# GpSimd's weight sums read the low parts from SBUF, and direct parts go to DRAM in the second plain block

## The chip, the core and the metric

The kernel runs on one core of one Trainium2 chip. The metric is the device time of one execution in microseconds (us); the median of several runs is compared. The engines are named as in the profile: PE is TensorE, ACT ScalarE, DVE VectorE, POOL GpSimd and SP SyncE, whose queue issues nearly all transfers here.

## The reference

```python
def _attn_ref(q, k, v):            # 8 x 8 heads, 576 tokens, 64 wide
    B, H, S, D = q.shape
    chunk = 64
    nc = S // chunk
    ...
    scores = scale * np.matmul(q_c, k_c.transpose(0, 1, 2, 4, 3))   # per chunk of 64
    scores = scores - np.max(scores, axis=-1, keepdims=True)
    attn = np.exp(scores)
    attn = attn / (np.sum(attn, axis=-1, keepdims=True) + 1e-09)
    out = np.matmul(attn, v_c)
...
def _moe_ref(x, w_in, w_out):      # x (4608, 512), w_in (512, 2048), w_out (2048, 512)
    h = x @ w_in
    g = np.where(h > 0.0, h, alpha * (np.exp(np.minimum(h, 0.0)) - 1.0))
    return (g @ w_out).astype(np.float32)
```

An attention within chunks of 64 tokens makes the 4608 x 512 matrix x; two matrix products with an ELU between them follow. The weights arrive as float64 words and are used as a high and a low float32r part, and x and g are split in the same way, so that each product is made of three matmuls (high by high, high by low, low by high).

## The kernel before

**Blocks.** The 4608 tokens are nine blocks of 512. The first three are computed plainly, block by block: for each of 16 column blocks f, h is computed (12 matmuls), put through the ELU, split, and multiplied with the rows f of w_out (12 matmuls). The other six blocks are taken two at a time, in three superblocks s = 0, 1, 2. In a superblock the first product is done by a scheme with seven products in place of eight: for each of eight pairs g of column blocks (2g and 2g + 1) the string PAIR lists the products (p1 to p7), their evacuations and sums (c, d), the steps of the ELU (digits), second products (Q), the steps of the attention of later tokens (m, E, z, h, q, k, s, v, x) and their loads (l, V). The first token block's half of g is used at once; the other half is kept in g_kept and multiplied with w_out afterwards, in the 16 rows of KEPT ("the second half-block"), where also the inputs of the next superblock are prepared (items beginning with x). The last superblock uses a scheme with seven products for w_out too.

**Order.** All engines work in the order in which the program issues to them; the strings are that order, written out by hand. An instruction that waits holds back all that stands behind it on its engine, and a transfer that waits holds back SP.

**The weights.** The operands for the seven products of w_in are written once to DRAM (a_dram, in `combine()`, during the second plain block) and loaded again for each pair (`load_a`, the profile's wi_hi<-a_dram; seven of 256 KB a pair). The high part of w_out stays in SBUF. Of the low part, from the third plain block on, only a ring of four slots is in SBUF, `weights[0][3]` (named wo_lo in the profile), each slot holding the low rows of two column blocks; `load_lo` reloads a slot of 512 KB from lo_dram, the copy in DRAM, once the second column block of the slot has been used, so that slot g is in the ring when pair g begins.

**Operands for the last superblock.** The seven operands made of w_out lie in b_dram. Three of them (A11, A12, A22) are plain parts of w_out. `write_direct` copies them in twelve transfers of 512 KB: six from SBUF (high parts, the profile's b_dram<-wo_hi) and six from lo_dram (low parts, DRAM to DRAM). The item w at the end of PAIR issues one of them per pair. The other four are sums. `Combination` makes them in 16 units (eight pairs g, two column halves m): load the low part from lo_dram into the tile quad (256 KB, line 556), add the high part on GpSimd (128x512), four sums of 128x128 on GpSimd (line 559), cast on ScalarE (line 572), subtract on VectorE (line 575), two writes to b_dram (line 581). Each item b in a string takes one of seven steps; the first 14 units are spread over the pairs of superblocks 0 and 1, the rest over KEPT of superblock 1 and the first pair of superblock 2.

The split of a kept column block (`split_kept`) casts on ScalarE and subtracts on GpSimd, except for column blocks 0 and 15, where VectorE subtracts.

Of the kernel before, what the change touches and what calls it, by code (L numbers as in the profile page):

```python
# [1 line left out]

# [1 line left out]

# [16 lines left out]
def kernel(  # L21
# [293 lines left out]
    class Later:  # L315


        def __init__(self, n: int):
            self.n = n
# [208 lines left out]
    HALF = DM // 2  # L528
    NM = HALF // P
    b_dram = dram.tile([NG, P, len(BOPS), 2, HALF], F32, name="b_dram")  # L530
    DIRECT = {"A11": (0, 0), "A12": (1, 0), "A22": (1, 1)}

    def write_direct(half: int, name: str, lo: int):
# [5 lines left out]
                "g p d -> p g d"),  # L539
            in_=src[:, :, e * DM + dh * HALF:e * DM + (dh + 1) * HALF])  # L540

    def quad_hi():
        return flat(weights[0][0])[:, NA * 4 * P:(NA + 1) * 4 * P]

    class Combination:

        def __init__(self, n: int):
            self.g, self.m = divmod(n, NM)
            half, f = divmod(2 * self.g, NF // 2)
            self.hi, self.lo = [  # L550
                w.rearrange("p (i m c) -> p i m c", i=4, m=NM)[:, :, self.m]
                for w in (flat(weights[half][2]).bitcast(F32)[:, f * DM:(f + 2) * DM],
                          lo_dram[half][:, f * DM:(f + 2) * DM])]

        def load(self):
            nc.sync.dma_start(out=quad, in_=self.lo)

        def pool(self, out, a, b, op):
            nc.gpsimd.tensor_tensor(out=out, in0=a, in1=b, op=op)  # L559

        def combine(self):
            a11, a21, a12, a22 = [quad[:, i] for i in range(4)]
            self.pool(quad, self.hi, quad, ALU.add)
            yield
            self.pool(a22, a21, a22, ALU.add)
            self.pool(a21, a11, a21, ALU.subtract)
            yield
            self.pool(a11, a22, a11, ALU.subtract)
            self.pool(a12, a12, a11, ALU.subtract)

        def cast(self):
            nc.scalar.copy(out=quad_hi(), in_=flat(quad))

        def subtract(self):
            nc.vector.tensor_tensor(
                out=flat(quad).bitcast(F32R), in0=flat(quad), in1=quad_hi().bitcast(F32),
                op=ALU.subtract)

        def write(self):
            for lo, src in enumerate((quad_hi().bitcast(F32), flat(quad))):  # L580
                nc.sync.dma_start(
                    out=b_dram[self.g, :, 3:, lo, self.m * P:(self.m + 1) * P],
                    in_=src.rearrange("p (i c) -> p i c", i=4))

    def combinations():
        for n in range(NG * NM):
            unit = Combination(n)
            unit.load()
            yield
            yield from unit.combine()  # L590
            yield
            for step in (unit.cast, unit.subtract, unit.write):
                step()
                yield

    def load_b(j: int):
        i, g = b_order[j]
# [201 lines left out]

    def split_kept(f: int):  # L800

        if f < NF - NTT or not preparing:
            hi, lo = [flat(weights[1][3])[:, (2 * (f % NTT) + i) * TB:(2 * (f % NTT) + i + 1) * TB]
                      for i in range(2)]
        else:
            hi, lo = g_tiles()
        for _ in split_g(g_place(f), hi, lo, nc.vector if f in (0, NF - 1) or not preparing and f % 2 == 0 else nc.gpsimd):
            pass
        second(f, hi, lo)

# [25 lines left out]
    def warm(n: int):  # L836
# [51 lines left out]
        "3 3"  # L888
    )
    SECOND_PAIR = (  # L890
        "p1 c1 5 5 h Q 4 p2 d1 4 Q q k p6 c2 1 Q Q 1 p5 1 1 Q l p7 c3 d2 Q Q 2 p4 c4 2 Q b 3 p3 "
        "d3 3 3 3 s v x V"
    )
    PAIR = (
        "b b b m p1 c1 4 E Q 4 z p2 d1 Q p6 c2 b h b 1 Q Q 1 p5 1 q k 1 b Q l p7 c3 d2 Q Q b 2 p4 c4 "
        "2 Q 3 p3 d3 3 3 3 s v x V w"
    )
    LAST_FIRST = (
        "b b b p1 c1 Q Q p2 d1 Q Q b b b p6 1 c2 Q p5 1 1 1 Q p7 c3 d2 Q Q 2 p4 c4 2 3 p3 d3"
    )  # L900
    LAST = (
        "5 4 p1 c1 Q 5 p2 4 t1 d1 Q 5 p6 1 t2 c2 p5 1 t3 1 1 th tl t4 p7 c3 d2 Q Q 2 p4 c4 2 3 p3 "
# [10 lines left out]
    )  # L913
    KEPT = (
# [145 lines left out]
    for f in range(NF):  # L1060
        tt, st = divmod(f, 4)
        n = 2 * NTT + tt + 1
        if st == 0:
            tile_now = following
            next(tile_now, None)
            next(tile_now, None)
            if tt == 0:
                later[n] = Later(n)
                later[n].load_qk()
            later[n].load_v()  # L1070
            following = later[n].steps()
        for item in (LATER if tt else SECOND_BLOCK)[st].split():
            if item == "H":
                act, acted = elu(hidden(f)), 0
            elif item == "e":
                g, acted = next(act), acted + 1
                if acted == 4:
                    second(f, *g)
            elif item == "a":
                next(tile_now, None)  # L1080
            elif item == "n":
                next(following, None)
            elif item == "X":
                if f == NF - 1:
                    split_next()
            elif item == "P":
                second_products()
            elif item == "S":
                store(*unstored.pop())
        if f < 2:  # L1090
            write_lo(NF - 2 + f)
        next(combining, None)
        if st == 2:
            later[n + 1] = Later(n + 1)
            later[n + 1].load_qk()
# [5 lines left out]
    def do(item: str):  # L1101
        if item == "Q":
            second_next()
        elif item == "b":
            next(combinations_next, None)
        elif item == "P":
            second_products()
        elif item == "S":
            store(*unstored.pop())
        elif item[0] == "x" and len(item) > 1:  # L1110
            if preparing:
                name, cols = item[1:3], slice(TB)
                if item[1] == "B":
                    name = item[1:4]
                elif item[3:4] in ("a", "b"):
                    cols = slice(T2) if item[3] == "a" else slice(T2, TB)
                prepare(name, cols)
# [5 lines left out]
    preparing = True  # L1123
# [20 lines left out]
    combinations_next = combinations()  # L1144
    direct_writes = iter([(half, name, lo) for half in range(2) for name in DIRECT for lo in range(2)])
# [50 lines left out]
    def pair_step(item: str, before):  # L1196
        if item[0] == "p":
            pair.product(int(item[1]))
        elif item[0] == "c":
            pair.keep(int(item[1]))  # L1200
        elif item[0] == "d":
            pair.add(int(item[1]))
        elif item in "45":
            if before:
                next(before.parts["3" if item == "5" else item], None)
        elif item in "123":
            next(pair.parts[item])
        elif item[0] == "t":
            before.combine(item[1])
        elif item == "w":  # L1210
            for what in [next(direct_writes, None)]:
                if what:
                    write_direct(*what)
        else:
            return False
        return True

    for s in range(NS):
# [5 lines left out]
        for g in range(NG):  # L1224
            before, pair = pair, Pair(s * NG + g)
            order = PAIR
            if last:
                order = LAST_FIRST if g == 0 else LAST_LAST if g == NG - 1 else LAST
            elif not s and g < 2:
                order = (FIRST_PAIR, SECOND_PAIR)[g]  # L1230
# [4 lines left out]
                    do(item)  # L1235
        if last:
            break
        preparing, kept = s + 2 <= NS - 1 or s + 1 < NS, iter(range(NF))
        run = n0 + TB, o_tiles(), b_half_place
        for line in KEPT:  # L1240
            for item in line.split():
                if item == "4":
                    next(pair.parts["4"], None)
                elif item == "G":
                    split_kept(next(kept))
                elif item == "B":
                    if s == NS - 2:
                        next(combinations_next, None)
                else:
                    do(item)  # L1250

# [48 lines left out]
```

## Time and profile before

| | us |
|---|---|
| median of 3 runs (lowest to highest) | 886.84 (886.29 to 888.61) |
| the profiled execution: time | 883.31 |
| its span, first to last instruction | 881.2 |
| TensorE busy | 831.8 (94%) |
| VectorE, ScalarE, GpSimd busy | 567.4, 506.4, 208.8 |
| granted TensorE clock over the span | 0.975 |

Some stretches of the span, as the trace shows them: start and attention of the first tokens to 28, the first plain block to 130, the second to 228, the third to 323, the pairs of superblock 0 to 478 and its KEPT to 523, the pairs of superblock 1 to 675 and its KEPT to 718, the last superblock to the end.

In a row of the trace "out<-in" names the tile written and the tile read, xN is the number of instructions merged, and the bracket at the end is the idle time before the instruction and what ended it. A row of a table by stretch gives the stretch and its length, then the busy time and number of instructions of each engine, the granted clock (1.00 is full), the mean busy share of the 16 DMA engines and the rate in GB/s. A row of waits gives who waited for whom, the total in us, the number of times and the longest. A row of a line or tile of SP gives the duration in ns (least, median, most) of issuing, and the times of the first and last.

### The profile page before, as it was taken

What the parts mean: (1) busy time and instruction counts of PE and PEld (TensorE: products, weight loads), DVE (VectorE), ACT (ScalarE), POOL (GpSimd) and SP (SyncE); (2) the same over time, 40 slices, a digit from 0 to 9 for tenths busy, and PEclk for the clock granted to TensorE, in tenths of its full rate; (3) what the DMA queues carried; (4) which work ended last, traced back from release to release, by engine and by line L of the source; (5) the groups of instructions that cost most, each with busy time, mean ns of one, the idle gap of its engine ahead of it and who ended that gap; (6) DMA issues with size and microseconds to landing.
All of it is one profiled execution on the core that took longest, in us unless ns stands there. A gap on an engine that the chain in (4) does not pass through costs nothing.

```text
span 881.2 us, 16030 instructions
## 1 busy us (share of the span) xinstructions
PE 831.8 (94%) x5901; PEld 674.4 (77%) x5901; DVE 567.4 (64%) x820; ACT 506.4 (57%) x910; POOL 208.8 (24%) x209
## 2 busy tenths in 40 slices
PE   6899999999899999698989999799899999999997
PEld 5787887888688878576867888577678888888886
DVE  4999986666755787454655766455555646777744
ACT  6999975444544457364645436445556447777641
POOL 0000004555012121222323463232224930000000
PEclk9999999999999999898999999989899999999999
DMA  9947965776785976599999868789987547665576
GB/s 248 274 149 228 297 146 167 239 233 194 230 212 153 239 187 207 156 279 254 264 259 262 250 165 251 222 245 255 262 242 215 172 134 242 195 193 158 153 211 150
DMA packets 231981, 189.29 MB, mean 215 GB/s; under 512 B 83936, under 2 KB 210400, under 8 KB 231904
## 3 DMA queue, kind: packets, MB, share of 16 engines
q1 hardware_dynamic: 229792, 188.01, 75.5%
q8 instruction: 47, 0.77, 0.4%
q10 hardware_dynamic: 2112, 0.26, 0.2%
q14 instruction: 30, 0.25, 0.1%
HBM read 144.70 MB, written 42.99 MB: 213 GB/s over the span
## 4 chain that ended last, share of the span: by engine, by line
PE 63%; DMA 11%; issue 9%; SPq 6%; ACT 5%; DVE 3%; POOL 3%; ACTq 0%; POOLq 0%
PE o L406 32%; PE h L406 27%; DMA b_dram<-lo_dram 3%; DMA quad<-lo_dram 2%; DMA wi_hi<-a_dram 2%; SPq L213 2%; POOL glo L441 2%; PE ps_a L233 1%; DMA b_dram<-wo_hi 1%; SPq L197 1%; PE ps_a L241 1%; POOL quad L559 1%; SPq L625 1%; DMA v_sb<-in_v_dram 1%; ACT unturned L367 1%
## 5 line engine op out<-in xcount | busy, mean ns | idle before, releaser
L406 PE MATMUL h<-xhi,wi_hi 128*128 128x512 f32 x324 | 116.3, 422 | 30.5 <-ACT kept L747 24.9
L406 PE MATMUL o<-wo_hi,ghi 128*128 128x512 f32 x352 | 140.8, 400 | 0.3 <-ACT k_sb L446 0.3
L406 PE MATMUL o<-wo_hi,glo 128*128 128x512 f32 x352 | 139.1, 395 | 1.1 <-DVE glo L441 0.6
L406 PE MATMUL o<-wo_lo,ghi 128*128 128x512 f32 x352 | 138.8, 394 | 0.0
L406 PE MATMUL h<-xlo,wi_hi 128*128 128x512 f32 x324 | 110.3, 402 | 0.0
L406 PEld LDWEIGHTS h<-xhi,wi_hi 128*128 128x128 f32 x324 | 63.8, 200 | 48.6 <-ACT kept L747 35.1
L682 POOL TENSOR_TENSOR glo<-e,ghi 128x512 fp32r<-128x512 f32 x32 | 41.4, 1293 | 167.8 <-ACT ghi L680 167.8
L406 PEld LDWEIGHTS o<-wo_hi,glo 128*128 128x128 f32 x352 | 67.1, 191 | 17.1 <-DVE glo L441 1.6
L406 PEld LDWEIGHTS o<-wo_hi,ghi 128*128 128x128 f32 x352 | 67.0, 190 | 15.2 <-ACT k_sb L446 0.4
L406 PEld LDWEIGHTS o<-wo_lo,ghi 128*128 128x128 f32 x352 | 67.1, 191 | 13.6
L406 PE MATMUL h<-wi_lo,wi_hi 128*128 128x512 f32 x288 | 75.1, 396 | 0.0
L406 PEld LDWEIGHTS h<-xlo,wi_hi 128*128 128x128 f32 x324 | 64.3, 199 | 13.9
L406 PE MATMUL h<-wo_lo,wi_hi 128*128 128x512 f32 x288 | 71.8, 389 | 0.0
L406 PE MATMUL o<-wo_hi,wo_lo 128*128 128x512 f32 x240 | 71.0, 390 | 0.0
L406 PE MATMUL h<-xhi,wi_lo 128*128 128x512 f32 x180 | 70.2, 390 | 0.0
L747 ACT COPY kept<-h 128x512 f32<-128x512 f32 x72 | 42.0, 583 | 40.9 <-PE h L406 40.7
L675 DVE SCALAR_TENSOR_TENSOR g_kept<-e,g_kept 128x512 f32<-128x512 f32 x48 | 34.9, 727 | 44.7 <-ACT e L672 44.7
L406 PEld LDWEIGHTS h<-wo_lo,wi_hi 128*128 128x128 f32 x288 | 54.0, 188 | 11.2
L672 ACT ACTIVATE e<-e 128x512 f32<-128x512 f32 x96 | 60.7, 632 | 3.1
L406 PEld LDWEIGHTS h<-wi_lo,wi_hi 128*128 128x128 f32 x288 | 52.9, 188 | 11.6 <-DVE g_kept L751 0.3
L406 PE MATMUL o<-wo_lo 128*128 128x512 f32 x192 | 59.9, 389 | 0.0
L751 DVE TENSOR_TENSOR g_kept<-h,kept 128x512 f32<-128x512 f32 x48 | 33.0, 688 | 36.8 <-PE h L406 30.1
(160 smaller groups left out, 1569.1 us busy)
## 6 DMA issues: line engine op xcount, KB each, us to landing
wi_hi<-a_dram SPq DMA_DIRECT2D x168, 256.0 KB, 4.3
wo_lo<-lo_dram SPq DMA_DIRECT2D x36, 512.0 KB, 5.6
wo_lo<-b_dram SPq DMA_DIRECT2D x56, 256.0 KB, 3.0
kept<-in_q_dram SPq DMA_DIRECT2D x100, 128.0 KB, 3.8
kept<-in_k_dram SPq DMA_DIRECT2D x100, 128.0 KB, 4.1
st<-in_moe_w_in_dram SPq DMA_DIRECT2D x16, 512.0 KB, 5.1
st<-in_moe_w_out_dram SPq DMA_DIRECT2D x16, 512.0 KB, 5.8
v_sb<-in_v_dram SPq DMA_DIRECT2D x32, 256.0 KB, 5.9
```

Of the source, the lines that this page charges most:

```text
L197: nc.sync.dma_start(out=dst[p0:p0 + n], in_=src[b, :, s0:s0 + n, :].rearrange("h s d -> s h d"))
L213: nc.sync.dma_start(out=qk[p0:p0 + n // U, w0:w0 + NK * U * D].rearrange("p (h w) -> p h w", h=NK), in_=src[b, j::2, s0:s0 + n, :].rearran ...
L233: nc.tensor.matmul(scores[halves[c], j, hp, :], lhsT=qT[halves[j], hp, halves[c]], rhs=kT[halves[j], hp, halves[c]], start=True, stop=True,)
L241: nc.tensor.matmul(x_ps[halves[j], c, hp, :], lhsT=v_sb[halves[c], 2 * hp + j, :], rhs=aT[halves[c], :, j * NK + hp], start=True, stop=True,)
L367: nc.scalar.copy(out=unturned, in_=turned)
L406: nc.tensor.matmul(ps, lhsT=a, rhs=b, start=start, stop=stop, skip_group_check=onto)
L441: engine.tensor_tensor(out=glo, in0=e, in1=ghi.bitcast(F32), op=ALU.subtract)
L672: nc.scalar.activation(out=e, in_=e, func=AF.Exp, scale=-1.0)
L675: nc.vector.scalar_tensor_tensor(out=to, in0=e, scalar=-1.0, in1=c, op0=ALU.add, op1=ALU.max)
L682: engine.tensor_tensor(out=lo, in0=e, in1=hi.bitcast(F32), op=ALU.subtract)
L747: nc.scalar.copy(out=c21 if i == 4 else self.kept[i - 1], in_=x_ps)
L751: nc.vector.tensor_tensor(out=to, in0=y_ps, in1=self.kept[kept], op=ALU.add)
```

## The change

The units of the sums no longer load quad. The first step adds the high part and the low part straight from the ring in SBUF; the unit (g, m = s) therefore runs within pair g of superblock s, while slot g is in the ring. The two units that have no pair (g = 0, 1 of superblock 0) run in KEPT of superblock 1, with tiles k_turned and quad for their sums and ghi and glo for their parts. A unit has six steps in place of seven. The twelve direct writes move from the pairs to the second plain block, one at the end of each of its column blocks 4 to 15. In KEPT of superblock 1 VectorE does all subtractions of the splits (before: two of 16). In KEPT of superblock 0 one step of an ELU comes two rows earlier (item D; L stands where it was, for superblock 1).

```diff
+    DIRECT_PARTS = [(name, lo) for name in ("A11", "A12", "A22") for lo in range(2)]
...
-    class Combination:
...
-        def load(self):
-            nc.sync.dma_start(out=quad, in_=self.lo)
...
-            self.pool(quad, self.hi, quad, ALU.add)
...
+    def combination(g: int, m: int, in_place: bool):
+
+        half, f = divmod(2 * g, NF // 2)
+        whi, wlo = [flat(w).bitcast(F32)[:, f * DM:(f + 2) * DM].rearrange(
+            "p (i m c) -> p i m c", i=4, m=NM)[:, :, m] for w in (weights[half][2], weights[0][3])]
+        sums = quad if in_place or g % 2 else k_turned
+        a11, a21, a12, a22 = [sums[:, i] for i in range(4)]
...
+        pool(sums, whi, wlo, ALU.add)
+        yield
+        pool(a22, a21, a22, ALU.add)
+        pool(a21, a11, a21, ALU.subtract)
+        yield
+        pool(a11, a22, a11, ALU.subtract)
+        pool(a12, a12, a11, ALU.subtract)
+        yield
+        hi, lo = (spare(), flat(sums).bitcast(F32R)) if in_place else g_tiles()
+        nc.scalar.copy(out=hi, in_=flat(sums))
+        yield
+        nc.vector.tensor_tensor(out=lo, in0=flat(sums), in1=hi.bitcast(F32), op=ALU.subtract)
+        yield
+        for i, src in enumerate((hi, lo)):
+            nc.sync.dma_start(
+                out=b_dram[g, :, 3:, i, m * P:(m + 1) * P],
+                in_=src.bitcast(F32).rearrange("p (i c) -> p i c", i=4))
+        yield
...
-        for _ in split_g(g_place(f), hi, lo, nc.vector if f in (0, NF - 1) or not preparing and f % 2 == 0 else nc.gpsimd):
+        on_vector = f in (0, NF - 1) or s == NS - 2
+        for _ in split_g(g_place(f), hi, lo, nc.vector if on_vector else nc.gpsimd):
...
     PAIR = (
-        "b b b m p1 c1 4 E Q 4 z p2 d1 Q p6 c2 b h b 1 Q Q 1 p5 1 q k 1 b Q l p7 c3 d2 Q Q b 2 p4 c4 "
-        "2 Q 3 p3 d3 3 3 3 s v x V w"
+        "b b b m p1 c1 4 E Q 4 z p2 d1 Q p6 c2 b h b 1 Q Q 1 p5 1 b q k 1 Q l p7 c3 d2 Q Q 2 p4 "
+        "c4 2 Q 3 p3 d3 3 3 3 s v x V"
     )
     LAST_FIRST = (
-        "b b b p1 c1 Q Q p2 d1 Q Q b b b p6 1 c2 Q p5 1 1 1 Q p7 c3 d2 Q Q 2 p4 c4 2 3 p3 d3"
+        "p1 c1 Q Q p2 d1 Q Q p6 1 c2 Q p5 1 1 1 Q p7 c3 d2 Q Q 2 p4 c4 2 3 p3 d3"
...
     KEPT = (
-        "4 m G E Q Q Q Q G",
-        "Q Q Q Q G z",
-        "Q Q h Q Q G 4 l",
-        "Q Q xB11 q k Q Q G",
-        "Q Q xB21 Q Q G B",
-        "Q Q Q Q s v x V G B",
-        "Q Q m xt1 Q Q E G B",
+        "4 m G E D Q Q Q Q G",
+        "Q Q Q Q G z b b b",
+        "Q Q h Q Q G L l",
+        "Q Q xB11 q k Q Q b b b G b b b",
+        "Q Q xB21 Q Q G",
+        "Q Q Q Q s v x V G",
+        "Q Q m xt1 Q Q E G b b b",
...
         if f < 2:
             write_lo(NF - 2 + f)
+        elif f >= 4:
+            write_direct(f % 2, *DIRECT_PARTS[(f - 4) // 2])
         next(combining, None)
...
+            if not last and (s or g >= 2):
+                combining = combination(g, s, True)
...
+            if s == NS - 2 and row == 0:
+                combining = chain(combination(0, 0, False), combination(1, 0, False))
```

More of the change, by code (lines that the diff above doesn't have):

```diff
@@ L1 @@
 from contextlib import ExitStack
+from itertools import chain
 import numpy as np
@@ L540, in write_direct @@
             in_=src[:, :, e * DM + dh * HALF:e * DM + (dh + 1) * HALF])
-    def quad_hi():
-        return flat(weights[0][0])[:, NA * 4 * P:(NA + 1) * 4 * P]
-    class Combination:
[L547 to L553, printed above, removed]
-        def load(self):
[L556 to L562, printed above, removed]
-            self.pool(quad, self.hi, quad, ALU.add)
[L564 to L594, printed above, removed]
+    def combination(g: int, m: int, in_place: bool):
[4 more added lines that the diff above has]
+        a11, a21, a12, a22 = [sums[:, i] for i in range(4)]
+        def pool(out, a, b, op):
+            nc.gpsimd.tensor_tensor(out=out, in0=a, in1=b, op=op)
+        pool(sums, whi, wlo, ALU.add)
[16 more added lines that the diff above has]
+        yield
@@ L596, in load_b, with spare @@
+    def spare():
+        return flat(weights[0][0])[:, NA * 4 * P:(NA + 1) * 4 * P]
     def load_b(j: int):
@@ L800, in split_kept @@
     def split_kept(f: int):
-        if f < NF - NTT or not preparing:
+        if f < NF - NTT:
             hi, lo = [flat(weights[1][3])[:, (2 * (f % NTT) + i) * TB:(2 * (f % NTT) + i + 1) * TB]
@@ L890 @@
     SECOND_PAIR = (
-        "p1 c1 5 5 h Q 4 p2 d1 4 Q q k p6 c2 1 Q Q 1 p5 1 1 Q l p7 c3 d2 Q Q 2 p4 c4 2 Q b 3 p3 "
-        "d3 3 3 3 s v x V"
+        "p1 c1 5 5 h Q 4 p2 d1 4 Q q k p6 c2 1 Q Q 1 p5 1 1 Q l p7 c3 d2 Q Q 2 p4 c4 2 Q 3 p3 d3 "
+        "3 3 3 s v x V"
     )
     PAIR = (
-        "b b b m p1 c1 4 E Q 4 z p2 d1 Q p6 c2 b h b 1 Q Q 1 p5 1 q k 1 b Q l p7 c3 d2 Q Q b 2 p4 c4 "
-        "2 Q 3 p3 d3 3 3 3 s v x V w"
+        "b b b m p1 c1 4 E Q 4 z p2 d1 Q p6 c2 b h b 1 Q Q 1 p5 1 b q k 1 Q l p7 c3 d2 Q Q 2 p4 "
+        "c4 2 Q 3 p3 d3 3 3 3 s v x V"
     )
     LAST_FIRST = (
-        "b b b p1 c1 Q Q p2 d1 Q Q b b b p6 1 c2 Q p5 1 1 1 Q p7 c3 d2 Q Q 2 p4 c4 2 3 p3 d3"
+        "p1 c1 Q Q p2 d1 Q Q p6 1 c2 Q p5 1 1 1 Q p7 c3 d2 Q Q 2 p4 c4 2 3 p3 d3"
     )
@@ L1104, in do @@
         elif item == "b":
-            next(combinations_next, None)
+            next(combining, None)
         elif item == "P":
@@ L1110, in do @@
         elif item[0] == "x" and len(item) > 1:
[L1111 to L1117, printed above, removed]
+            name, cols = item[1:3], slice(TB)
+            if item[1] == "B":
+                name = item[1:4]
+            elif item[3:4] in ("a", "b"):
+                cols = slice(T2) if item[3] == "a" else slice(T2, TB)
+            prepare(name, cols)
         elif item[0] == "A":
@@ L1121, in do @@
             attention.step(item)
-    preparing = True
     run = (PLAIN - 1) * TB, o_tiles(), b_half_place
@@ L1143 @@
     k_flat = flat(k_turned)
-    combinations_next = combinations()
-    direct_writes = iter([(half, name, lo) for half in range(2) for name in DIRECT for lo in range(2)])
+    combining = iter(())
     turned_order = [item for item in TURNED.split() if item in "65743"]
@@ L1209, in pair_step @@
             before.combine(item[1])
[L1210 to L1213, printed above, removed]
         else:
@@ L1237 @@
             break
-        preparing, kept = s + 2 <= NS - 1 or s + 1 < NS, iter(range(NF))
+        kept = iter(range(NF))
         run = n0 + TB, o_tiles(), b_half_place
-        for line in KEPT:
+        for row, line in enumerate(KEPT):
+            if s == NS - 2 and row == 0:
+                combining = chain(combination(0, 0, False), combination(1, 0, False))
             for item in line.split():
@@ L1245 @@
                     split_kept(next(kept))
-                elif item == "B":
-                    if s == NS - 2:
-                        next(combinations_next, None)
+                elif item in "DL":
+                    if (s < NS - 2) == (item == "D"):
+                        next(pair.parts["4"], None)
+                elif item == "b":
+                    next(combining, None)
                 else:
```

4 rows, old and new, of the table KEPT are left out of this document.

## The prediction

> **What bounds the kernel now.** I read the page first, then cut the span into stretches and pairs, then the waits of the slow stretches, then one slow pair and one undisturbed pair engine by engine.
>
> ```profile
> span 881.2 us, 16030 instructions
> PE 831.8 (94%) x5901; PEld 674.4 (77%) x5901; DVE 567.4 (64%) x820; ACT 506.4 (57%) x910; POOL 208.8 (24%) x209
> ...
> PE o L406 32%; PE h L406 27%; DMA b_dram<-lo_dram 3%; DMA quad<-lo_dram 2%; DMA wi_hi<-a_dram 2%; SPq L213 2%; POOL glo L441 2%; PE ps_a L233 1%; DMA b_dram<-wo_hi 1%; SPq L197 1%; PE ps_a L241 1%; POOL quad L559 1%; SPq L625 1%; DMA v_sb<-in_v_dram 1%; ACT unturned L367 1%
> ```
>
> TensorE is busy 94% of the span, so a gain must come from the few places where it is not. The chain that ended last names three transfers that this change touches: the two kinds of direct write (b_dram from lo_dram, b_dram from wo_hi) and the load of quad. Where they sit is told by the stretches, cut at the first matmul of a pair: pairs 2 to 7 of superblock 0, a free pair and a slow pair of superblock 1, pairs 2 to 7 of superblock 1, and the last of them alone.
>
> ```profile
> core 0: us, PE busy (x) PEld busy (x) DVE busy (x) ACT busy (x) POOL busy (x), PEclk, DMA share, GB/s
> 354.33:478.04 123.71, 106.94 (x787) 85.00 (x781) 64.89 (x103) 62.33 (x108) 34.62 (x42) 0.92 0.90 245
> 539.16:555.44 16.28, 16.28 (x136) 13.34 (x131) 10.86 (x18) 10.45 (x18) 6.07 (x7) 1.00 0.86 262
> 580.14:600.32 20.18, 18.17 (x137) 14.39 (x131) 10.78 (x18) 10.34 (x18) 5.72 (x7) 0.92 0.93 257
> 555.44:674.71 119.27, 105.59 (x754) 83.89 (x748) 62.94 (x100) 62.34 (x108) 34.62 (x42) 0.93 0.86 242
> 658.90:674.71 15.81, 15.81 (x104) 12.87 (x98) 9.02 (x15) 10.45 (x18) 6.05 (x7) 1.00 0.69 204
> ```
>
> The free pair takes 16.28 us with TensorE never idle. Six such pairs would be 97.7 us, where superblock 0 takes 123.71: 26.0 us lost. In superblock 1 five at 16.28 and the light last one at 15.81 would be 97.2 of 119.27: 22.1 lost. Together 48.1 us, idle time and slowed clock (0.92 and 0.93) alike. Everything the change can win lies there. Who waits there is in the waits of superblock 0's six pairs:
>
> ```profile
> POOL quad L559 <- DMA quad<-lo_dram: 26.2, 6, 8.9
> ...
> PE h L406 <- ACT kept L747: 16.8, 5, 7.2
> ```
>
> Read from below: TensorE waits for ScalarE's evacuation (kept), and GpSimd waits in every pair for the load of quad. The link between them shows in one slow pair (first matmul at 580.14; SP, POOL, ACT and PE rows), and then in the free pair (first matmul at 539.16).
>
> ```profile
> 580.24 0.60 SPq L556 DMA_DIRECT2D quad<-lo_dram  x1
> 581.56 0.54 SPq L641 DMA_DIRECT2D wo_lo<-lo_dram  x1
> 581.23 1.30 POOL L682 TENSOR_TENSOR glo<-e,ghi 128x512 fp32r<-128x512 f32 x1 [7.43 <-ACT ghi L680]
> 586.21 1.29 POOL L559 TENSOR_TENSOR quad<-wo_hi,quad 128x512 f32<-128x512 f32 x1 [3.69 <-DMA quad<-lo_dram]
> 587.58 2.08 POOL L559 TENSOR_TENSOR quad<-quad 128x128 f32<-128x128 f32 x4
> 585.91 0.59 ACT L747 COPY kept<-h 128x512 f32<-128x512 f32 x1 [1.81 <-PE h L406]
> 589.69 0.62 ACT L572 CAST wi_hi<-quad 128x512 fp32r<-128x512 f32 x1 [3.20 <-DMA b_dram<-wo_hi]
> 594.00 1.19 PE L406 MATMUL h<-xhi,wi_hi 128*128 128x512 f32 x4 [2.01 <-ACT kept L747]
> ...
> 541.72 1.29 POOL L559 TENSOR_TENSOR quad<-wo_hi,quad 128x512 f32<-128x512 f32 x1 [0.17 <-DMA quad<-lo_dram]
> 543.09 2.40 POOL L559 TENSOR_TENSOR quad<-quad 128x128 f32<-128x128 f32 x4
> 545.53 0.62 ACT L572 CAST wi_hi<-quad 128x512 fp32r<-128x512 f32 x1
> ```
>
> In the slow pair the add stands 3.69 us for the load; GpSimd ends at 587.58 + 2.08 = 589.66 and ScalarE's cast starts 0.03 us later. The row puts that wait down to a transfer into b_dram, but GpSimd's end fits to the hundredth, so I take it as the releaser. Behind the cast, in ScalarE's order, stand the ELU and the evacuation that TensorE needs. In the free pair the load had landed, and the cast starts as soon as ScalarE reaches it. The cast stands 6.37 us after the pair's start there and 9.55 us in the slow pair: 3.18 us late makes 2.01 us of idle TensorE, so about 1.2 us of lateness is free.
>
> **The change, part by part.** *The load of quad goes.* The ring slot of pair g was filled turns earlier, so the add waits for GpSimd's own split alone. In the slow pair that ends at 581.23 + 1.30 = 582.53; with the free pair's 3.77 us for the five sums (541.72 to 545.49) they end at 586.30, and ScalarE comes to the cast at 585.91 + 0.59 = 586.50. The wait is gone with 0.2 us to spare and 1.2 us behind it. What is late next is nothing in that pair: the free pair shows the same order with the cast unblocked. The new reader also holds back the slot's reload on SP, but the slot is reloaded a pair after the sum has read it, (SP's row at 581.56 stands 1.4 us after its pair's start, the sum's read a whole pair before it), so that wait is covered by more than 10 us; if the cover went, the loads of a_dram queued behind it on SP would come late.
>
> *The direct writes leave the pairs.* Six pairs of superblock 0 moved 245 GB/s x 123.71 us = 30.3 MB. A load of 262 KB and a direct write of 524 KB less per pair leaves 25.6 MB, 4.26 MB a pair. At full engines (245 / 0.90 = 272 GB/s) that is 15.7 us, just under 16.28; at the plain 245 it is 17.4. The free pair itself ran at 262 GB/s with a share of 0.86, the rate that 4.26 MB in 16.28 us asks for, so I go by it and allow 0.3 us a pair for lateness, 3.6 us over twelve (ends 0 and 13.4). Two pairs, one in each superblock, load a tile that crosses a batch boundary:
>
> ```profile
> 551.61 4.12 SPq L213 DMA_DIRECT2D kept<-in_q_dram  x8
> 555.77 5.14 SPq L213 DMA_DIRECT2D kept<-in_k_dram  x8
> ...
> 575.39 2.23 SPq L213 DMA_DIRECT2D kept<-in_q_dram  x4
> 577.66 1.85 SPq L213 DMA_DIRECT2D kept<-in_k_dram  x4
> ```
>
> That is 9.3 us of SP in place of 4.1; between 0 and 5.2 us stay lost in each, and I take 1.5, 3 us in all.
>
> *The direct writes arrive in the second plain block*, one at the end of each of the last twelve column blocks. What they cost SP and the DMA engines, the stretches they come into, and what hangs on SP at that block's end (SP and PE rows):
>
> ```profile
> L537 SPq DMA_DIRECT2D b_dram<-wo_hi x6: 791/1028/2326, 382.7 to 624.3; - x6
> L537 SPq DMA_DIRECT2D b_dram<-lo_dram x6: 623/1326/1721, 402.1 to 643.8; - x6
> ...
> DMA to landing us min/median/max: 6.3/7.0/8.0
> ...
> 155.00:192.00 37.00, 37.00 (x223) 30.51 (x222) 23.75 (x32) 16.95 (x27) 19.05 (x19) 1.00 0.71 228
> 192.00:228.60 36.60, 36.60 (x278) 29.78 (x277) 24.54 (x35) 17.73 (x29) 18.83 (x18) 1.00 0.70 214
> ...
> 205.49 2.41 SPq L371 DMA_DIRECT2D turned<-unturned  x4
> ...
> 233.61 2.47 SPq L371 DMA_DIRECT2D turned<-unturned  x4
> ...
> 237.58 0.79 PE L241 MATMUL ps_a<-turned,v_sb 64*64 64x64 f32 x32 [1.53 <-ACT ps_a L348]
> ```
>
> TensorE is busy throughout and has cover to lose. The DMA engines have 0.29 x 37.0 + 0.30 x 36.6 = 21.7 us free; twelve writes of 524 KB at 272 GB/s take 23.1, at this block's own 228 / 0.71 = 321 GB/s 19.6. So they just fit, with later landings. From 205.49 to the transfers of turned at 233.61 SP's 43 issues take 26.0 of 28.1 us. Four writes fall in that run: two at 1.03 and two at 1.33 us, 4.7 less about 1 us of gap that they find; the product with v at 237.58, which started within a few tenths of when these transfers can have landed, moves with them. I take 4 us (ends 0, if the landings are early enough, and 17, below). The sums of the first weights in this block bear a late landing: GpSimd ends one at 159.31 + 3.51 = 162.82, ScalarE needs it at 170.56.
>
> ```profile
> 159.31 3.51 POOL L471 TENSOR_TENSOR kept<-kept 128x256 f32<-128x256 f32 x4
> ...
> 170.56 1.04 ACT L499 CAST kept<-kept 128x1024 fp32r<-128x1024 f32 x1
> ```
>
> *The second half-block (KEPT) of superblock 1.* Fourteen splits move from GpSimd to VectorE, the sums of pairs 0 and 1 come in, and the last steps of the sums leave the next superblock's first pair. They are half as wide as the row of 1.25 us below, so I put them at 0.8 us at most, 11 us in all. TensorE is never idle there and VectorE has 23.79 of 43.60 us busy, so I cost it at nothing; if splits queue behind the 1024-wide preparations, one of these (1.2 us) could show at a few rows, 3 us at most. Moving one ELU step of superblock 0's KEPT two rows forward costs nothing: TensorE is full there too (45.00 of 45.00).
>
> ```profile
> 478.00:523.00 45.00, 45.00 (x264) 37.11 (x257) 31.97 (x34) 21.00 (x33) 23.47 (x16) 1.00 0.81 227
> 674.70:718.30 43.60, 43.60 (x200) 36.11 (x193) 23.79 (x18) 19.42 (x29) 29.19 (x21) 1.00 0.52 165
> 682.76 4.54 DVE L660 TENSOR_TENSOR wi_lo<-xf,wi_lo 128x1024 fp32r<-128x1024 f32 x2
> 707.79 1.25 DVE L660 TENSOR_TENSOR wo_lo<-xf,wo_lo 128x1024 fp32r<-128x1024 f32 x1 [6.68 <-PE o L406]
> ```
>
> **Sum.** -48.1 + 3.6 + 3 + 4 = -37.5 us. The profiled execution took 883.31 us (span 881.2), so 845.8 for such a one; it lies 3.5 us below the median of the runs, so the median goes from 886.84 to 849.3.
>
> **The rivals.**
> *Transfers still bound the pairs.* Share 0.90 speaks for it, the free pair against it. At 17.4 us a pair: 849.3 - 3.6 + 13.4 = 859.
>
> *The second plain block overflows.* Six of the writes go from DRAM to DRAM; if each costs its time twice, 23.1 + 11.6 = 34.7 us meet 21.7 free, 13 us too much, and with the 4 of SP 17 in place of 4: 862. For it: no row prices such a write alone. Against it: the 272 GB/s come from pairs that hold them. The Trainium skill ("DMA: Bandwidth & Descriptors", Queues, rings and completion order) has each engine take the descriptors of a ring in order, which speaks against this change: the small transfers of turned would stand behind 512 KB. By that rule the transfers of turned would land up to 1.9 us later still and the sum would be 851; by the rows alone it stays 849, and the trace of before has no such pair of transfers in this block.
>
> *The sums are stretched.* They now run in every pair while VectorE works. The last fence has VectorE at 4.54 / 2 = 2.27 us, in a KEPT where GpSimd works too, for what takes 1.25. At twice 3.45 the sums end at 589.4, the cast is 2.9 us late as before, and all but the clean start is given back: some 40 us, 889. Against it: the free pair's sums ran beside VectorE in 3.77. The Trainium skill ("GPSIMD Engine Reference", Key points) says that GpSimd shares its SBUF interfaces with VectorE and contends with instructions of two SBUF inputs; the KEPT rows agree, the free pair's hardly, and 849 goes by the latter.
>
> *The sums wait all the same,* for the newest reload of the ring and not for their own slot's. It is issued at 581.56, 1.3 us after quad's load, so the stalls would stay (20.18 us for such a pair): about 889.
>
> *Slower:* each direct write puts its landing of 7.0 us on TensorE's path in the second plain block, through SP, late sums and ScalarE's order: 12 x 7.0 = 84, so 849.3 - 4 + 84 = 929. It ends above before from 3.5 us a write on; the 7.7 us of cover above speak against it.
>
> **Chances and range.** Forecast 0.62 (its own range 841 to 858), bound pairs 0.13, overflow 0.13, stretched sums 0.04, waiting sums 0.04, slower 0.04. A measurement of this kernel tells about 0.3%, 2.7 us, from no change. The two cases at 889 lie at that bound: half same, half slower. Faster 0.88, same 0.04, slower 0.08. The range goes from 839 (all 48.1 won) to 870 (overflow and bound pairs together: 872).
>
> **What would show it.** Right: no wait of quad for a transfer; ScalarE's cast without idle time before it; pairs of 16.3 to 16.8 us with a clock of 1.00; in the second plain block a DMA share near 1 and a gap of some 4 us before the product with v at its end. Wrong: TensorE still waiting for kept in the pairs, pairs above 17 us with a share near 1, or gaps spread through the second plain block.

## The result and the profile after

The changed kernel took 854.49 us (median; 852.06 to 863.12) against 886.98 before: the ratio of the times, taken over all runs and not from the two medians, is 0.9649, 95% interval 0.9576 to 0.9722. A second measurement gave 855.72 against 888.80, 0.9642 (0.9614 to 0.9670). So 32 to 33 us were won where 37.5 were forecast. The profiled execution of the first four was the slowest of them, 863.12 us, span 861.3; a second profile has a span of 852.3. Both are read below, since they differ in places that teach something.

The wait for the load of quad, on which the prediction rests, is gone. In a pair of superblock 0 GpSimd adds right behind its split, and ScalarE's cast starts without idle time (rows of POOL and ACT, changed kernel):

```profile
398.48 1.29 POOL L663 TENSOR_TENSOR glo<-e,ghi 128x512 fp32r<-128x512 f32 x1 [5.53 <-ACT ghi L661]
399.73 1.30 POOL L553 TENSOR_TENSOR quad<-wo_hi,wo_lo 128x512 f32<-128x512 f32 x1
401.11 2.42 POOL L553 TENSOR_TENSOR quad<-quad 128x128 f32<-128x128 f32 x4
403.65 0.62 ACT L564 CAST wi_hi<-quad 128x512 fp32r<-128x512 f32 x1
```

The five sums take 399.73 to 403.53, 3.80 us, as in the free pair of before. What TensorE and GpSimd wait for is told by the waits from 130 to 720 us, the kernel before, then the changed kernel's first and second profile:

```profile
PE h L406 <- ACT kept L747: 24.9, 9, 7.2
```

```profile
PE ps_a L242 <- DMA turned<-unturned: 15.0, 12, 5.7
...
PEld ps_a L242 <- DMA turned<-unturned: 10.9, 14, 2.5
...
POOL quad L553 <- DMA b_dram<-quad: 9.1, 5, 4.3
...
PEld h L407 <- ACT kept L728: 1.1, 2, 0.6
```

```profile
PE ps_a L242 <- DMA turned<-unturned: 9.9, 8, 5.2
...
PEld ps_a L242 <- DMA turned<-unturned: 5.3, 7, 1.6
...
POOL quad L553 <- DMA b_dram<-quad: 3.6, 3, 1.6
```

Before, TensorE waited 24.9 us for kept and never for turned; now it waits for turned, the four small transfers between the softmax of a tile and its product with v. GpSimd's add still waits for a transfer in some pairs, those of superblock 1 above all: not for a load, but until the last unit's results have been written out of the tile quad. In the second profile nothing waited for these sums in turn; in the first, ScalarE's cast did twice, 2.6 us in all.

The stretches below are cut at the products with v (rows ps_a<-turned of PE), and the last two at the first matmul of superblock 2, so that they bear the same work in every kernel; the table gives us from the profiles.

| stretch | before | after, 1st profile | after, 2nd profile |
|---|---|---|---|
| to the first product with v of the second block | 148.1 | 149.8 | 151.4 |
| second block to the third's second tile | 100.0 | 108.5 | 106.9 |
| the rest of the third block, pairs 0 and 1 | 105.7 | 106.0 | 106.0 |
| pairs 2 to 7 of superblock 0 | 123.7 | 101.1 | 97.7 |
| its second half-block and pair 0 | 61.1 | 66.0 | 61.1 |
| pairs 1 to 7 of superblock 1 | 135.5 | 122.8 | 121.9 |
| its second half-block | 44.3 | 44.3 | 44.4 |
| the rest | 162.8 | 162.8 | 162.9 |

The second profile sums to -28.9 us: -26.0 in superblock 0's pairs, -13.6 in superblock 1's, +6.9 at the second block's end. The first line differs by up to 3.5 us between profiles of kernels in which nothing was changed ahead of it (147.9 to 151.4). In superblock 0 the second profile shows the pairs as free as pairs can be, and the first one not (stretches of the first, then of the second):

```profile
364.25:465.34 101.09, 99.43 (x793) 80.97 (x785) 64.50 (x104) 62.75 (x108) 36.50 (x42) 1.00 0.93 247
465.34:531.36 66.02, 63.58 (x387) 51.97 (x390) 37.71 (x43) 29.86 (x48) 27.59 (x21) 0.97 0.74 210
```

```profile
364.30:461.98 97.68, 97.68 (x793) 80.00 (x788) 63.99 (x103) 62.80 (x108) 36.23 (x42) 1.00 1.00 264
461.98:523.10 61.12, 61.12 (x399) 50.32 (x394) 39.35 (x44) 29.71 (x48) 28.63 (x21) 1.00 0.77 214
523.10:645.03 121.93, 116.33 (x892) 94.23 (x883) 73.02 (x117) 73.48 (x126) 42.50 (x49) 1.00 0.85 230
```

97.68 us with TensorE never idle is six times 16.28, at a DMA share of 1.00. In the first profile the first two of these pairs take 16.28 us as well and the other four 16.9 to 17.4; what set them off is not known. A share of 1.00 is no fixed rate: the third tile of the second block (196.72 to 220.07 us of the first profile) has 1.01 at 309 GB/s.

Most of the loss at the second block's end is one wait (SP, DVE and PE rows, first profile):

```profile
226.94 3.67 SPq L214 DMA_DIRECT2D kept<-in_k_dram  x8
...
232.98 1.06 DVE L333 STREAM_TRANSPOSE qT<-kept 128x512 f32<-128x512 f32 x1
...
237.39 1.76 SPq L214 DMA_DIRECT2D kept<-in_q_dram  x4
239.19 1.85 SPq L214 DMA_DIRECT2D kept<-in_k_dram  x4
241.15 1.34 SPq L198 DMA_DIRECT2D v_sb<-in_v_dram  x2
242.58 2.47 SPq L372 DMA_DIRECT2D turned<-unturned  x4
...
245.71 0.45 PE L242 MATMUL ps_a<-turned,v_sb 64*64 64x64 f32 x2 [5.75 <-DMA turned<-unturned]
```

The transfers of turned left SP at 233.61 before and leave it at 242.58 now, 9.0 us later, of which 1.7 are the later start of this profile. Ahead of the loads at 237.39 SP itself stood 2.3 us (1.0 before) until writes from their tile (a_dram<-kept) had landed, and turned stands behind these loads. The wait also has a price behind it: the 12.5 us from 245.71 to the third block's second tile had a granted clock of 0.77 (second profile: 11.8 us, 0.83), where before they were 10.5 us at 1.00.

### The profile page after: what moved, and what is told of

The parts are those of the page before. It is cut to its first block, busy times and chain, and to the rows that moved or that the text cites. A ratio compares the mean times of both kernels' runs of the same rounds, so it can differ in the third digit from the quotient of the medians.

```text
span 861.3 us, 16013 instructions
## 1 busy us (share of the span) xinstructions
PE 829.2 (96%) x5901; PEld 673.2 (78%) x5901; DVE 573.7 (67%) x834; ACT 507.7 (59%) x910; POOL 190.7 (22%) x195
## 4 chain that ended last, share of the span: by engine, by line
PE 68%; DMA 11%; issue 8%; SPq 4%; ACT 4%; DVE 3%; POOL 2%; POOLq 0%; ACTq 0%
PE o L407 33%; PE h L407 30%; DMA turned<-unturned 4%; PE ps_a L242 2%; DMA wi_hi<-a_dram 2%; POOL glo L442 2%; DMA st<-in_moe_w_out_dram 1%; SPq L372 1%; SPq L198 1%; SPq L214 1%; PE ps_a L234 1%; PE h L424 1%; DMA wo_lo<-lo_dram 1%; DMA b_dram<-quad 1%; DVE glo L442 1%
## 5 line engine op out<-in xcount | busy, mean ns | idle before, releaser
L407 PE MATMUL h<-xhi,wi_hi 128*128 128x512 f32 x324 | 109.0, 397 | 0.2 <-ACT kept L728 0.2
L407 PE MATMUL h<-xlo,wi_hi 128*128 128x512 f32 x324 | 107.5, 392 | 0.1
L407 PEld LDWEIGHTS o<-wo_hi,glo 128*128 128x128 f32 x352 | 66.1, 188 | 16.8 <-DVE glo L442 2.1
L407 PEld LDWEIGHTS h<-xhi,wi_hi 128*128 128x128 f32 x324 | 61.2, 189 | 14.1 <-ACT kept L728 1.1
L407 PEld LDWEIGHTS h<-xlo,wi_hi 128*128 128x128 f32 x324 | 61.2, 189 | 12.9 <-issue 0.5
L407 PEld LDWEIGHTS o<-wo_hi,wo_lo 128*128 128x128 f32 x240 | 45.8, 191 | 10.0 <-DVE kept L447 0.2
```

The source lines that it names most:

```text
L407: nc.tensor.matmul(ps, lhsT=a, rhs=b, start=start, stop=stop, skip_group_check=onto)
```

## The experiments

**Which half of the change won the time.** One kernel has the ring and leaves the direct writes in the pairs, the other moves them and keeps the load of quad.

```diff
# ring_only, against the changed kernel
-        elif f >= 4:
-            write_direct(f % 2, *DIRECT_PARTS[(f - 4) // 2])
...
     PAIR: "... 3 3 3 s v x V"  ->  "... 3 3 3 s v x V w"
```

> The sums read the ring, the direct writes stay in the pairs. Theory 1 (the pairs stood still because the add waited for its load, and ScalarE's cast behind it): the cast has no wait over 1 us, pairs 2 to 7 of superblock 0 take 100 to 108 us in place of 123.7, the second plain block is as before, 848 to 858 us. Theory 2 (the pairs were bound by the bytes moved, and quad is a third of what leaves them): a third of the gain, 870 to 876 us, pairs 113 to 118 us.

```diff
# direct_only, against the kernel before
         if f < 2:
             write_lo(NF - 2 + f)
+        elif f >= 4:
+            write_direct(f % 2, *[(name, lo) for name in DIRECT for lo in range(2)][(f - 4) // 2])
...
     PAIR: "... s v x V w"  ->  "... s v x V"
```

> The direct writes go to the second plain block, the sums still load quad. Theory 1: ScalarE's cast still waits in most pairs (over 1.5 us), pairs of superblock 0 take 115 to 122 us, the second plain block and the start of the third lose 5 to 10 us, 878 to 888 us. Theory 2: two thirds of the gain in the pairs, 107 to 112 us, 862 to 870 us in all.

ring_only: 869.23 us, ratio 0.9787 (0.9763 to 0.9811). direct_only: 895.84 us, 1.0087 (1.0061 to 1.0114), 0.9% slower than before. Pairs 2 to 7 of superblock 0 and what TensorE or ScalarE waited for there, ring_only and then direct_only:

```profile
355.90:463.74 107.84, 101.56 (x793) 82.44 (x785) 65.19 (x104) 63.68 (x109) 37.66 (x43) 0.98 0.93 255
...
PEld ps_a L242 <- DMA turned<-unturned: 7.0, 6, 2.4
PE ps_a L242 <- DMA turned<-unturned: 6.3, 5, 2.3
```

```profile
364.90:491.76 126.86, 108.68 (x793) 86.14 (x788) 64.73 (x103) 62.20 (x108) 34.59 (x42) 0.91 0.83 218
...
ACT wi_hi L572 <- POOL quad L559: 25.3, 6, 9.5
PE h L406 <- ACT kept L747: 18.2, 5, 8.3
```

With the direct writes out of the pairs and the load of quad still in, the share of the DMA engines falls to 0.83 and the pairs do not get faster at all (126.86 us, 123.70 before). The load of quad lands no sooner either (median 5.7 us after its issue, 5.8 before). So the wait for the load made the stalls, and not the number of bytes. Both theories' numbers for direct_only missed (pairs of 115 to 122 or 107 to 112 us, 878 to 888 or 862 to 870 in all); the wait itself is as Theory 1 has it. With the load out and the direct writes in, the cast no longer waits, the pairs win 15.9 us, and the last four stop at 18.4 to 19.0 us each, at the waits for turned; 869 is a miss for both theories' times (848 to 858, 870 to 876), and 107.84 lies in Theory 1's range for the pairs. Alone the parts give -19.6 and +7.0 us; together -33.1. Moving the writes is worth 13.5 us, but only once the load is gone.

**The price of the writes in the second block.**

```diff
# no_direct, against the changed kernel
-        elif f >= 4:
-            write_direct(f % 2, *DIRECT_PARTS[(f - 4) // 2])
...
-            in_=b_dram[g, :, BOPS.index(PRODUCTS[i][0])].rearrange("p l d -> p (l d)"))
+            in_=b_dram[g, :, max(3, BOPS.index(PRODUCTS[i][0]))].rearrange("p l d -> p (l d)"))
```

> The changed kernel without the twelve direct writes (the last superblock loads parts of the sums in their place, so that the same bytes are loaded). It prices the writes in the second plain block. Theory 1 (they delay the transfers of turned at the block's end through SP and the DMA queue): the wait of 5.75 us is gone, the stretch from the second plain block to the third's second column block is 7 to 9 us shorter than in the changed kernel's profile, 843 to 849 us. Rival (the wait comes from the load of the tile that crosses a batch, not from the writes): the wait stays over 3 us and the time within 3 us of the changed kernel's.

847.48 us, 0.9547 (0.9513 to 0.9581). The stretch from the second block to the third's second tile takes 100.76 us: the wait for turned is gone, and the writes cost 6 to 8 us there. Next comes where they stand:

```diff
# spread, against the changed kernel: six in the second block, six in the third
-        elif f >= 4:
+        elif 4 <= f < 10:
...
+        if 2 <= f < 8:                       # in the third block's loop
+            write_direct(f % 2, *DIRECT_PARTS[3 + (f - 2) // 2])
         next(combining, None)
```

> The changed kernel with the same twelve direct writes at other places: six at the ends of column blocks 4 to 9 of the second plain block, six at 2 to 7 of the third. SP is free of them from column block 10 to the second block's end. If SP's lateness there made the wait for turned, it is under 1 us and the stretch to the third block's second tile is 5 to 8 us shorter: 847 to 851 us. If it is the bytes in flight, half of it stays: 851 to 855 us.

851.60 us, 0.9595 (0.9563 to 0.9626); the stretch takes 101.09 us and the wait for turned at the block's end is gone, as the first theory has it, though the time lies 0.6 us outside its range. The third block takes 1.4 us more than in the changed kernel. Against no_direct the two stretches together are 1.6 us longer: that is what the same bytes cost here, in place of 6 to 8 us. This run does not tell SP's issues from the bytes in flight, since both left the block's end; turned_mixed, below, does.

**What is left in the pairs.** Three tries on the transfers of turned, and two that change the load on SP and on the DMA engines one at a time.

```diff
# turned_act, against the changed kernel
-                    nc.sync.dma_start(out=turned[to, 1 - e], in_=unturned[of, e])
+                    nc.scalar.dma_start(out=turned[to, 1 - e], in_=unturned[of, e])
```

> The changed kernel with the four transfers of turned per tile issued on ScalarE's queue in place of SP's. Theory A (what is left of the stalls is these transfers, late behind SP's other issues): no wait of TensorE for turned over 0.3 us in the pairs and none of 5 us at the second plain block's end; if issuing on ScalarE costs about what it costs SP (0.58 us each), ScalarE comes 2.3 us late to the evacuations and some of it returns as waits for kept: 845 to 856 us. Rival B (the DMA engines are simply full): turned lands as late as before, 854 to 860 us.

938.72 us, 1.0561 (1.0532 to 1.0590). Each tile holds ScalarE for the four issues (its rows):

```profile
429.27 2.44 ACTq L372 DMA_DIRECT2D turned<-unturned  x4
431.75 0.63 ACT L652 ACTIVATE e<-c 128x512 f32<-128x512 f32 x1 [2.52 <-DMA turned<-unturned]
```

The waits for turned are gone, but 2.4 us of lateness on ScalarE is past the 1.2 us that the prediction worked out as free, and superblock 0's pairs take 18.4 to 23.6 us. From 130 to 760 us TensorE now waits 20.4 us for kept, as the expectation had it, but also 20.4 us for loads of a_dram and 14.8 us for the transposes into k_turned, which it did not have. It underrated the price by far, and why the loads of a_dram came late is open.

```diff
# a_late, against the changed kernel
+                held.append((self.g + 1, i))          # in place of load_a(self.g + 1, i)
+                if not holding:
+                    issue_held()
...
+                if item == "h":                       # behind the transfers of turned
+                    holding = False
+                    issue_held()
```

> The changed kernel, where SP issues the next pair's loads of a_dram for products 1, 2 and 6 behind the transfers of turned and not ahead of them. Theory A: turned leaves SP about 3 us earlier, the pairs of both superblocks take 16.3 to 16.8 us and the waits for turned in them are under 0.3 us; the second plain block stays, 842 to 850 us. Rival B (full DMA engines): turned is issued earlier and lands 3 us or more after issue all the same, pairs stay at 17 to 18 us in superblock 1, 853 to 858 us.

864.42 us, 0.9712 (0.9675 to 0.9748), slower than the change and outside both forecasts. In superblock 0 the waits for turned are gone and others have come (POOL and ACT rows of one pair, then the SP rows that follow):

```profile
384.93 1.29 POOL L553 TENSOR_TENSOR quad<-wo_hi,wo_lo 128x512 f32<-128x512 f32 x1 [2.33 <-DMA b_dram<-quad]
...
388.42 0.62 ACT L564 CAST wi_hi<-quad 128x512 fp32r<-128x512 f32 x1 [1.84 <-POOL quad L553]
...
390.20 2.47 SPq L372 DMA_DIRECT2D turned<-unturned  x4
392.77 3.44 SPq L606 DMA_DIRECT2D wi_hi<-a_dram  x4
396.26 0.59 SPq L569 DMA_DIRECT2D b_dram<-wi_hi  x1
396.95 0.46 SPq L569 DMA_DIRECT2D b_dram<-quad  x1
```

The held loads now stand ahead of quad's writes to b_dram, these land late, and the next pair's add waits for the tile and the cast for the add. That is the old chain from another end, but TensorE's own waits in these pairs are mostly for the held loads themselves (2.3 us for a_dram, 0.8 behind ScalarE's ELU). The wait at the second block's end is there too, 7.1 us.

```diff
# half_lo, against the changed kernel (load_lo)
-            out=weights[0][3][:, f:f + 2, :].bitcast(F32),
+            out=weights[0][3][:, f:f + 2, :HALF].bitcast(F32),
...
# a_in_two, against the changed kernel (load_a)
+        for l in range(2):                            # two transfers of 128 KB in place of one
+            nc.sync.dma_start(out=a_place(i - 1)...[:, l], in_=a_dram[g % NG, :, l, AOPS.index(name)])
```

> The changed kernel, where each reload of the ring brings only the left half of its columns: 262 KB a pair less, as many transfers (the right half keeps older low parts). Theory S (what is left of the stalls is SP, whose issues fill the pair): superblock 1's pairs take 121 to 123 us as in the changed kernel, 852 to 857 us in all. Rival B (the bytes in flight): they take 113 to 117, superblock 0 runs at 16.28 us a pair in every profile, 842 to 849 us.

> The changed kernel, where each load of a_dram is issued as two transfers of 128 KB: the same bytes, seven more issues a pair on SP. Theory S: seven issues of 0.4 to 0.55 us make each pair 1 to 3 us longer in both superblocks, 865 to 895 us. Rival B: pairs as before, 852 to 860 us.

half_lo: 845.20 us, 0.9552 (0.9536 to 0.9569), superblock 1's pairs 114.6 us in place of 121.9. a_in_two: 873.39 us, 0.9877 (0.9856 to 0.9899), superblock 0's pairs 108.5 and superblock 1's 125.8. Fewer bytes help and more issues hurt, so neither theory alone holds (a_in_two also halves the size of each transfer, which this run does not tell from the added issues). A link is in SP's rows after the tile that crosses a batch, in the changed kernel (second profile) and in half_lo:

```profile
549.28 2.95 SPq L606 DMA_DIRECT2D wi_hi<-a_dram  x3
552.33 3.87 SPq L372 DMA_DIRECT2D turned<-unturned  x4
```

```profile
546.79 1.89 SPq L606 DMA_DIRECT2D wi_hi<-a_dram  x3
548.77 2.47 SPq L372 DMA_DIRECT2D turned<-unturned  x4
```

The same seven issues take 6.82 us and 4.36 us: with the larger reloads issuing itself gets longer, SP falls behind, and turned leaves late. Why an issue gets longer is open. It is not the load on the DMA engines at that moment, since their share during the seven issues is 0.98 in the changed kernel (549.28 to 556.20 us) and 1.05 in half_lo (546.79 to 551.24).

```diff
# turned_pool, against the changed kernel
-                    nc.sync.dma_start(out=turned[to, 1 - e], in_=unturned[of, e])
+                    nc.gpsimd.dma_start(out=turned[to, 1 - e], in_=unturned[of, e])
```

> The changed kernel with the transfers of turned issued by GpSimd. SP has four issues less a tile (2.4 us) and they no longer stand behind its other transfers. Theory S: no wait for turned of over 1 us in the pairs or at the second plain block's end, pairs at 16.3 us in both superblocks, 838 to 848 us, if GpSimd's issuing hides in its idle time. If GpSimd's issuing holds back its splits by more than their slack, TensorE waits for glo and the time is 855 to 880 us.

887.53 us, 1.0024 (1.0013 to 1.0035), outside both ranges: both mechanisms of the expectation are there at once, and the second costs more than forecast. Superblock 0's pairs take 97.68 and superblock 1's 114.7, and the wait at the second block's end is gone; but the third block takes 36 us more, since its splits stand on GpSimd behind the wait for ScalarE (waits from 258 to 375 us):

```profile
POOL turned L372 <- ACT unturned L368: 74.8, 6, 14.6
...
PE o L407 <- POOL glo L442: 23.1, 6, 4.0
```

**A better version.** GpSimd issues these transfers only where its splits do not stand behind them.

```diff
# turned_mixed, against the changed kernel
+    def queue_of_turned(n: int):
+        return nc.gpsimd if n == PLAIN * NTT or n >= 20 and n not in (27, 28) else nc.sync
...
+                    queue_of_turned(self.n).dma_start(out=turned[to, 1 - e], in_=unturned[of, e])
```

> The changed kernel with the transfers of turned issued by GpSimd only where its splits do not stand behind them: for the tile at the second plain block's end and for those of the pairs; in the plain blocks otherwise and in the second half-block of superblock 0 SP issues them. If SP's lateness is all that is left in these places, each stretch is the best one seen so far: second block to the third's second tile 101 to 102 us, third 106, superblock 0's pairs 97.7, its half-block 61.1, superblock 1's pairs 114.7: 840 to 845 us. If GpSimd's issuing disturbs the sums in the pairs (as the third block's splits), 850 us and more.

841.83 us, 0.9484 (0.9461 to 0.9508), as forecast and better than both kernels. The stretches are 101.4, 106.0, 97.7, 61.1 and 114.4 us; superblock 0's and 1's pairs:

```profile
356.21:453.89 97.68, 97.68 (x793) 80.00 (x788) 63.93 (x103) 62.71 (x108) 48.22 (x66) 1.00 0.99 266
515.01:629.40 114.39, 113.92 (x891) 93.12 (x882) 72.78 (x117) 73.21 (x126) 56.27 (x77) 1.00 0.92 248
```

The transfers of turned land in 3.4 us (median), no sooner than in the changed kernel (3.3). So it is their issue that was late, not their landing that was long. The second block's stretch takes 101.4 us with all twelve direct writes still in it, so what they cost there (6 to 8 us) came from turned's place behind them in SP's order, and not from their bytes. The run moves turned to another engine and takes its issues off SP at once; which of the two counts for more in the pairs is not told apart. The Trainium skill ("DMA: Bandwidth & Descriptors", Issuing engines are not separate DMA queues) says that issuing from several engines saves only the sequencer's time for issuing, usually small. The runs agree that the landing is not shortened; the saving was not small here, 13.9 us between the medians (855.72 to 841.83).

**The splits in superblock 1's second half-block.**

```diff
# split_pool, against the changed kernel
-        on_vector = f in (0, NF - 1) or s == NS - 2
+        on_vector = f in (0, NF - 1)
```

> The changed kernel with the splits of the second half-block of superblock 1 on GpSimd again (14 of 16). The prediction costed that move at nothing, 3 us at most: this half-block takes 43.5 to 44.5 us and the time is within 2 us of the changed kernel's. If the move mattered, the half-block is over 1 us longer here.

860.97 us, 0.9677 (0.9644 to 0.9711). The half-block takes 46.56 us where the changed kernel takes 44.36 (the second profile); its stretch, and then that of the changed kernel (columns: us, busy us and instructions of PE, PEld, DVE, ACT and POOL, the clock, the DMA share and GB/s):

```profile
650.48:697.04 46.56, 44.57 (x226) 36.62 (x225) 26.35 (x19) 19.67 (x31) 32.16 (x25) 1.00 0.51 155
```

```profile
645.03:689.39 44.36, 44.36 (x226) 36.62 (x225) 29.72 (x33) 20.03 (x31) 10.47 (x11) 1.00 0.55 165
```

2.2 us from this part of the change; the rest of the difference between the two medians lies within what the runs of one kernel differ by. The half-block was over 1 us longer, so the move mattered, as the second half of the expectation has it. With GpSimd busy 32 of 46 us VectorE is slowed (the same subtraction takes 2.31 us in split_pool and 1.23 in the changed kernel, DVE rows in this order):

```profile
679.03 2.31 DVE L641 TENSOR_TENSOR xlo<-xf,xlo 128x1024 fp32r<-128x1024 f32 x1
```

```profile
669.27 1.23 DVE L641 TENSOR_TENSOR xlo<-xf,xlo 128x1024 fp32r<-128x1024 f32 x1 [0.26 <-ACT xlo L640]
```

**The kernel once more.**

> The changed kernel once more, with five rounds and a second profile. Expected 850 to 858 us. If the 4.5 us lost in the second half-block of superblock 0 and the wait of 5.75 us before the product with v at the end of the second plain block are properties of the kernel and not of one execution, both are in this profile too (each over 2 us).

855.72 us. The 4.9 us of the second half-block of superblock 0 are not in the second profile, the wait at the second block's end is (5.2 us): the first belongs to an execution whose pairs had fallen behind, the second to the kernel. The other kernels bear this out where SP issues turned and the sums read the ring: the half-block with pair 0 takes 61.1 us where superblock 0's pairs took 97.7 or 97.8 (half_lo, spread), and 63.6 to 67.4 us where they took over 100 (five kernels).

## Why the prediction was right, point by point

*The chain through quad, ScalarE's cast and kept:* right. direct_only shows it with the bytes gone and the load there, and the changed kernel has 1.1 us of TensorE's waits for kept left. One wait was overlooked: the add does not wait for GpSimd's own split alone, but also until the tile quad has been written out (up to 4.3 us). So the sign "no wait of quad for a transfer" holds in superblock 0 of the second profile and fails in superblock 1.

*Superblock 0's pairs:* forecast 26.0 less 1.8 and 1.5, so -22.7; measured -22.6 and -26.0. The crossing tile cost nothing there in the second profile.

*Superblock 1's pairs:* the mis-sized term. Forecast -18.8, measured -12.7 and -13.6. The crossing pair loses 3.0 us, not 1.5, and what was allowed for lateness, 0.3 us a pair, is 0.5 to 1.8 in the four pairs behind it (18.04, 17.59, 16.81 and 17.25 us in the second profile). What the step missed is that the transfers stay late for several pairs once SP has fallen behind. With fewer bytes (half_lo) or with turned off SP (turned_mixed) the pairs are back at 16.28 us from the second one behind the crossing pair. The sign of 16.3 to 16.8 us a pair fails here, and two of the pairs are above 17.5 us at a DMA share of 0.90 and 0.92, near what was to show the forecast wrong; the clock is 1.00, as forecast.

*The writes in the second block:* forecast 4 us, measured 8.4 and 6.9 (first and second profile); 6 to 8 against no_direct. The place and the gap were right: the tile that ends with the wait is 5.4 and 4.3 us longer. What the sum left out is 1.0 and 1.4 us in the tiles ahead of it, and 2.0 and 1.2 us behind it at the lower clock. The working of the gap was right in its sum more than in its parts (first profile against before): the four writes took SP 3.1 us, not 4.7, but other issues beside them got 1.4 us longer, and SP's wait for the landing of a_dram<-kept 1.3 us longer.

*The second half-block of superblock 1, costed at nothing:* the move of the splits is worth 2.2 us, which offsets the added sums there (44.4 against 44.3 before).

*The number.* 32 to 33 us in place of 37.5 is in part luck: in the second profile the terms for superblock 1 and for the second block were 5.2 and 2.9 us too good, and superblock 0 came out 3.3 us better than forecast.

*The rivals.* Pairs bound by bytes: refuted as the cause before (direct_only), but bytes are part of what holds the pairs after (half_lo). Overflow: the DMA share of the second block rose from 0.74 to 0.88 with no gap of TensorE as long as 1 us ahead of its end (first profile); the price lies at its end. By the Trainium skill's rule on the order within a ring ("DMA: Bandwidth & Descriptors", Queues, rings and completion order) turned should land later behind larger transfers. The median went from 1.9 to 3.3 us, which agrees in direction; but in turned_mixed the 60 transfers that GpSimd issues go through a queue of their own and land in 4.0 us, so these runs do not show the order behind SP's transfers to be the reason. Stretched sums: refuted in the pairs (3.80 us against 3.77), seen in superblock 1's half-block (an add of 2.27 us in place of 1.30), where nothing was lost by it. Waiting sums: refuted, the add waits for no reload. The slower case: no engine waited for a sum of the first weights, though GpSimd's own waits for their writes to land went from 20.4 to 36.4 us.

## What to carry over

Look for the instruction that stands in an engine's order between a late transfer and the bound engine; its wait can be worth more than the bytes of the transfer, and moving bytes alone can even cost. When such a stall goes, look next at the engine that issues: count its issues per turn, and measure how long they take in place, since the same ones can take half as long again. Give short transfers with a deadline to a queue whose engine is idle at that time and has nothing urgent behind them.

## What the runs showed of the hardware

A DMA share of 1.00 at 264 GB/s over 97.7 us went with a TensorE that was never idle, and so did 1.01 at 309 GB/s over 23.4 us. Seven issues of SP took 4.36 us in half_lo and 6.82 us in the changed kernel, at about the same DMA share. Four issues took ScalarE 2.44 us and GpSimd 2.07. After a wait of 5.75 us TensorE's granted clock averaged 0.77 over the next 12.5 us; before the change, after a wait of 1.53 us at the same place, it was 1.00. VectorE's 128x1024 subtraction took 1.23 us alone and 2.31 beside a busy GpSimd.
